# The output row in two 224-column halves on two column groups, and the last output weights in another order

## The chip, the cores and the metric

The kernel runs on one core of one Trainium2 chip. The metric is the device time of one execution in microseconds (us). Runs were made in sets of rounds: in each set the kernel before was run too, and a kernel is compared with the runs of the kernel before in its own set, because the kernel before itself has medians from 1284.22 to 1284.88 us in different sets. A ratio is the mean time of one kernel's runs over that of the other's of the same rounds, so it is not quite the ratio of the medians quoted beside it.

## The reference, cut to what matters

One token attends to a long cache, and a gated feed-forward branch is mixed in.

```python
# x: 1x448; k_cache, v_cache: 8 kv heads x 65536 x 256, bf16; wq: 448x4096; wo: 4096x448
q = (x @ wq) as 16 heads of 256           # 2 q heads share one kv head
p = softmax(q k^T / 16);  o = p v
a = o.reshape(4096) @ wo                  # 1x448
h = relu(x @ W_gate) * (x @ W_up)         # 1x1792
b = h @ W_down                            # 1x448
out = g * a + (1 - g) * b,  g = sigmoid(sum(x * gate_w))
```

The two caches are 2 x 268 MB, read once. Everything else is small.

## The kernel before: the parts that matter

K and V come in tiles of 8 MB (128 partitions x 64 KB) into a ring of three buffers. The order of the transfers on the one DMA queue is fixed by a list. The first K tile goes to buffer 0, the feed-forward weights to buffer 2, the second K tile to buffer 1. The third K tile needs buffer 2, so it can be issued only after the feed-forward products have been computed.

```python
order = [("wq", 0, 8.7), ("k", 0, TILE), ("gu", 0, 7.7), ("wd", 0, 3.8)]
for n in range(1, NT):
    order.append(("k", n, TILE))
    ...
slot, held, freed = {}, {2: ["gu", "dn"]}, {}      # buffer 2 is free after products gu and dn
...
PIECES = [(0, 64), (64, 96), (96, 112), (112, 120), (120, 128)]   # the last V tile in five pieces
for i, (lo, hi) in enumerate(PIECES):
    order.append(("vp", i, TILE * (hi - lo) / U))
WO = [(JL, 2 * NW), (2 * NW, J - 4), (J - 4, J - 2), (J - 2, J - 1), (J - 1, J)]
for i in range(1, 5):
    order.append(("wo", i, 0.55 * (WO[i][1] - WO[i][0])))
```

The w_down product (called dn) is 14 matmuls of one row by 448 columns. It opens the sum for the output row. The wo product closes it: per q head two matmuls, one in row 0 and one in row 32 of the same PSUM bank, except for the last head, where both go to row 0. ScalarE copies row 32 out early, and VectorE adds the two.

```python
def f_dn(e):
    for ft in range(FT):
        ins = e.matmul(A_ps[0:1, 0:D], hT[:, ft:ft + 1], wd_sb[:, ft, :], start=(ft == 0), ...)
...
r_ = 32 if s == 1 and j < J - 1 else 0
ins = e.matmul(A_ps[r_:r_ + 1, 0:D], attnT[:, c:c + 1], wo_sb[:, j, s, :], ..., tile_position=(0, r_))
...
f0 = op("ac", ..., lambda e: e.copy(a_sb, A_ps[32:33, 0:D]), ...)
f1 = op("dv", T_END, lambda e: e.tensor_tensor(fin_o, A_ps[0:1, 0:D], a_sb, ALU.add), [fin, f0])
```

The first three heads (JL = 3) use another layout of the attention output (attnL) and of the weights, which are loaded by eight transfers to 4 partitions each:

```python
for f in range(2):
    for i_ in range(4):
        dma(... wl_sb[32 * f + i_:32 * f + i_ + 13:4, :, :], wlv[f, i_] ...)
```

Of the kernel before, what the change touches and what calls it, by code (L numbers as in the profile page):

```python
# [7 lines left out]
F32 = mybir.dt.float32  # L8
# [4 lines left out]
ALU = AluOpType  # L13
# [11 lines left out]
class _Plan:  # L25
# [8 lines left out]
    def op(self, eng, key, fn, deps=()):  # L34
        o = _Op(eng, key, fn, deps)
        self.ops.append(o)
        return o

    def dma(self, eng, key, sem, fn, deps=()):
        if sem not in self.dsem:  # L40
            self.dsem[sem] = self.es.enter_context(self.nc.semaphore("d_" + sem))
        o = _Op(eng, key, fn, deps, dma=sem)
        self.ops.append(o)
        return o
# [46 lines left out]
def bass_gated_mix__gqa_block_cached__glu_gated_reglu__decode_kernel(  # L91
# [13 lines left out]
    H = A_k_cache.shape[1]  # L105
    S = A_k_cache.shape[2]
    DH = A_k_cache.shape[3]
    D = A_x.shape[2]
    F = B_W_gate.shape[1]
    NQ = A_wq.shape[1]  # L110
    J = 2 * H
# [11 lines left out]
    JL = 3  # L123
# [4 lines left out]
    with es:  # L128
# [5 lines left out]
        ptp = [sb("ptp%d" % i, [128, 1024], BF) for i in range(2)]  # L134
# [18 lines left out]
        attnT = sb("attnT", [128, H * 4], BF)  # L153
        attnL = sb("attnL", [128, 32], BF)
        hT = sb("hT", [128, FT], BF)
# [7 lines left out]
        fin_o = P_sb[0:1, 0:D]  # L163
        gw_row = ptp[1][0:1, 0:D]
        xeo = ptp[1][0:1, 448:704]
        qrep = ptp[1][:, 704:960]
        a_sb = ptp[H % 2][0:1, 0:2 * D].bitcast(F32)
        gtmp = ptp[0][0:1, 0:2 * D].bitcast(F32)

        wq3 = ring[2][:, 0:R3 * NQ]  # L170
# [6 lines left out]
        wd_sb = ring[2][:, 0:FT * D].rearrange("p (ft d) -> p ft d", ft=FT)  # L177
# [4 lines left out]
        A_ps = ps("A_ps", [128, 512], F32)  # L182
# [12 lines left out]
        op, dma = pl.op, pl.dma  # L195
# [9 lines left out]
        order = [("wq", 0, 8.7), ("k", 0, TILE), ("gu", 0, 7.7), ("wd", 0, 3.8)]  # L205
# [4 lines left out]
        NW = H - 3  # L210
# [2 lines left out]
        order.append(("wl", 0, 0.5))  # L213
        order.append(("wo", 0, 7.3))
        PIECES = [(0, 64), (64, 96), (96, 112), (112, 120), (120, 128)]
        for i, (lo, hi) in enumerate(PIECES):
            order.append(("vp", i, TILE * (hi - lo) / U))

        WO = [(JL, 2 * NW), (2 * NW, J - 4), (J - 4, J - 2), (J - 2, J - 1), (J - 1, J)]
        for i in range(1, 5):  # L220
            order.append(("wo", i, 0.55 * (WO[i][1] - WO[i][0])))
        t = 3.0
        tL, issue = {}, []
        for kind, i, d in order:
# [3 lines left out]
        T_END = t + 20.0  # L228
# [9 lines left out]
        wo_sb = ring[slot["wl", 0]][:, 0:J * 2 * D].rearrange("p (j s n) -> p j s n", j=J, s=2)  # L238
        wl_sb = ring[slot["wl", 0]][:, J * 2 * D:(J * 2 + JL * 8) * D].rearrange("p (j m) -> p j m", j=JL)
# [104 lines left out]
        def f_qk(n, b, sl):  # L344
# [12 lines left out]
                return ins  # L357
            return f

        l_, qk, smax, aexp, pv, last = {}, {}, {}, {}, {}, {}  # L360
        pending = []

# [61 lines left out]
        for kind, i, t in issue:  # L424
# [34 lines left out]
            elif kind == "wd":  # L459
                a3 = dma("sp", t, "wd", lambda e: e.dma_start(wd_sb, B_W_down.rearrange("(p ft) d -> p ft d", ft=FT)), [l_["q"]])  # L460

                def f_dn(e):
                    for ft in range(FT):
                        ins = e.matmul(A_ps[0:1, 0:D], hT[:, ft:ft + 1], wd_sb[:, ft, :], start=(ft == 0), stop=False,
                                       skip_group_check=True)
                    return ins
                l_["dn"] = op("pe", max(tg + 12.2, tL["wd", 0]), f_dn, [l_["hT"], a3])
            elif kind == "k":
# [14 lines left out]
                if t_ == NTH - 1:  # L483
# [12 lines left out]
                    ev = []  # L496
# [61 lines left out]
                        l_["wl"] = dma("sp", t + 0.01 * (4 * f + i_), "wl", lambda e, f=f, i_=i_: e.dma_start(  # L558
                            wl_sb[32 * f + i_:32 * f + i_ + 13:4, :, :], wlv[f, i_]), free(("wl", 0)))


        LAST = last["tn", H - 1]
        def f_wl(e):
            for j in range(JL):
                for s in range(8):
                    c = j // 2 * 16 + s * 2 + j % 2
                    ins = e.matmul(A_ps[0:1, 0:D], attnL[0:48, c:c + 1], wl_sb[0:48, j, s * D:(s + 1) * D],
                                   start=False, stop=False, skip_group_check=True, tile_position=(0, 0))
            return ins
        op("pe", max(tL["wo", 0], last["tn", NW - 1] + 0.5), f_wl,  # L570
           [l_["wl"], l_["dn"]] + [last["norml", h] for h in range((JL + 1) // 2)])
        for i, (lo, hi) in enumerate(WO):
            for h in range(lo // 2, (hi + 1) // 2):
                key = max(tL["wo", i], last["tn", h] + 0.5) + 0.01 * h
                if i in (1, 2):
                    key = LAST - (0.7, 0.2)[i - 1]
                elif i > 2:
                    key = LAST + 2 + 0.1 * i

                def f_wo(e, h=h, lo=max(lo, 2 * h), hi=min(hi, 2 * h + 2)):  # L580
                    for j in range(lo, hi):
                        for s in range(2):
                            c = h * 4 + s * 2 + j - 2 * h
                            r_ = 32 if s == 1 and j < J - 1 else 0
                            ins = e.matmul(A_ps[r_:r_ + 1, 0:D], attnT[:, c:c + 1], wo_sb[:, j, s, :],
                                           start=(s == 1 and j == JL), stop=(j == J - 1 or (j == J - 2 and s == 1)),
                                           skip_group_check=True, tile_position=(0, r_))
                    return ins
                fin = op("pe", key, f_wo, [l_["wo", i], last["norm", h], l_["dn"]])
                if i == 3:  # L590
                    f0 = op("ac", key + 0.01, lambda e: e.copy(a_sb, A_ps[32:33, 0:D]), [fin, last["ev", H - 2][1]])
        f1 = op("dv", T_END, lambda e: e.tensor_tensor(fin_o, A_ps[0:1, 0:D], a_sb, ALU.add), [fin, f0])
        f2 = dma("sp", T_END + 1, "out", lambda e: e.dma_start(out[0, :, :], fin_o), [f1])

        pl.serialize(touch_m)
        progs = pl.finish()
# [53 lines left out]
```

## Time and profile before

| what | value |
|---|---|
| median of 3 runs | 1284.27 us (1284.11 to 1284.40) |
| bytes read | 549 MB, mean 429 GB/s |
| busiest compute engine | VectorE, 49% |
| third K tile issued | 61.30 us |
| first piece of the last V tile: wait ends | 1266.19 us |
| output DMA issued | 1281.01 us |

From the page of the kernel before: the span from the first to the last instruction, engine busy time, then the row of the 40 slices for the DMA engines (9 is 90% or more) and the line of the main DMA queue.

```profile
span 1282.5 us, 10004 instructions
...
PE 431.5 (34%) x4636; PEld 163.4 (13%) x4636; DVE 634.4 (49%) x426; ACT 61.8 (5%) x116; POOL 4.1 (0%) x21
...
DMA  9999999999999999999999999999999999999998
...
q1 hardware_dynamic: 12674, 549.03, 99.3%
```

The reader sees a kernel bound by its transfers. No compute engine is near full. The Trainium skill (Perfetto Trace Analysis, "What 'DMA-bound' means") lists "Specific DMA engines" as the first thing that such a kernel can be bound on. This case agrees: the trace keeps 16 completion times for the last wo transfer, and they reach from 1271.27 to 1279.38. The mean over all 16 hides it.

Now the tail, from the timeline of the kernel before. Columns: start, duration, engine, line, operation, output<-inputs, shapes, count, and in brackets the idle time before it and what ended it.

```profile
1266.19 3.58 PE L376 MATMUL O<-ring,ptp 128*4 128x512 bf16 x32 [3.41 <-DMA ring<-in_A_v_cache_dram]
...
1274.81 0.60 PE L376 MATMUL O<-ring,ptp 128*4 128x512 bf16 x4 [0.21 <-DMA ring<-in_A_v_cache_dram]
1276.07 0.60 PE L376 MATMUL O<-ring,ptp 128*4 128x512 bf16 x4 [0.66 <-DMA ring<-in_A_v_cache_dram]
1276.72 0.69 DVE L387 CAST o_sb<-O 128x512 bf16<-128x512 f32 x1 [56.13 <-PE O L376]
...
1277.17 0.91 PE L585 MATMUL A_ps<-ring,attnT 128*1 128x448 bf16 x4 [0.50 <-DMA ring<-in_A_wo_dram]
...
1278.01 0.27 PE L392 MATMUL M_ps<-emat,o_sb 128*128 128x2 bf16 x4
...
1278.30 2.03 PE L585 MATMUL A_ps<-ring,attnT 128*1 128x448 bf16 x8
1278.31 0.16 DVE L396 TENSOR_TENSOR attnT<-M_ps,hs 128x4 bf16<-128x4 f32 x1 [0.90 <-PE M_ps L392]
...
1279.42 0.09 PEld L585 LDWEIGHTS A_ps<-ring,attnT 128*1 128x1 bf16 x2 [0.48 <-DMA ring<-in_A_wo_dram]
1279.62 0.52 ACT L591 COPY ptp<-A_ps 1x448 f32<-1x448 f32 x1 [59.15 <-PE A_ps L585]
1280.36 0.61 DVE L592 TENSOR_TENSOR P_sb<-A_ps,ptp 1x448 bf16<-1x448 f32 x1 [1.89 <-PE A_ps L585]
1281.01 0.28 SPq L593 DMA_DIRECT2D out_dram<-P_sb  x1
```

The last V piece is waited for until 1276.07. The normalised output of the last kv head (attnT) is ready at 1278.47. But the last wo head lands only at 1279.42, and after it come 1.59 us: matmuls, add, issue. So the last wo transfer ends the kernel.

And the start, from the timeline around 60 us (the SPq row is the issue of the third and fourth K tile):

```profile
58.46 2.81 PE L464 MATMUL A_ps<-ring,hT 128*1 128x448 bf16 x14
61.30 0.80 SPq L472 DMA_DIRECT2D ring<-in_A_k_cache_dram  x2
```

The issue follows the w_down product at once.

The table of stretches at the end of the kernel before (columns: stretch, its length, busy time and count of each engine, granted clock, DMA share, GB/s):

```profile
1277.00:1278.00 1.00, 0.83 (x4) 0.09 (x4) 0.41 (x1) 0.00 (x0) 0.00 (x0) 0.50 0.27 104
1278.00:1279.00 1.00, 0.98 (x11) 0.35 (x10) 0.16 (x1) 0.00 (x0) 0.00 (x0) 0.50 0.08 29
```

A share of 0.08 of 16 engines is one or two engines. Seven packets are in flight at 1277.0, three at 1278.0 and none at 1279.0, so a few stragglers set the last landing.

### The profile page before, as it was taken

To read this page: it belongs to the slowest core of one execution; us is meant where nothing else is said; L and a number is where in the kernel's file an instruction comes from. 1 tells how busy PE (TensorE), PEld (TensorE's weight loads), DVE (VectorE), ACT (ScalarE), POOL (GpSimd) and SP (SyncE) were. 2 spreads that over 40 slices of the span, in tenths; PEclk is the share of its full clock that TensorE was granted. 3 is DMA by queue.
4 is the path that set the end of the run, shared out by engine and by line. 5 is a ranking of instruction groups with operands and counts; after the bars stand their busy time and mean duration, and the time that the engine had idled before them with its cause. 6 is when DMAs were issued, how large, how long until landed. Compare 5 with 4: busy or idle time off the path is not lost.

```text
span 1282.5 us, 10004 instructions
## 1 busy us (share of the span) xinstructions
PE 431.5 (34%) x4636; PEld 163.4 (13%) x4636; DVE 634.4 (49%) x426; ACT 61.8 (5%) x116; POOL 4.1 (0%) x21
## 2 busy tenths in 40 slices
PE   3633332334123431225331243321433324233236
PEld 2401110111001110001110111100111101011011
DVE  2597633465534655434555444555435555335600
ACT  0001000000000000000000000000000000000000
POOL 1000000000000000000000000000000000000000
PEclk9656666656566665666655666656666655666576
DMA  9999999999999999999999999999999999999998
GB/s 398 424 426 436 440 427 432 443 427 426 438 440 430 428 430 437 434 434 424 436 438 432 427 438 436 426 429 444 430 426 434 438 431 430 440 428 432 436 413 328
DMA packets 12719, 549.67 MB, mean 429 GB/s; under 512 B 1315, under 2 KB 3238, under 8 KB 3718
## 3 DMA queue, kind: packets, MB, share of 16 engines
q1 hardware_dynamic: 12674, 549.03, 99.3%
q8 instruction: 36, 0.59, 0.2%
q14 instruction: 5, 0.04, 0.0%
q10 hardware_dynamic: 4, 0.00, 0.0%
HBM read 549.03 MB, written 0.00 MB: 428 GB/s over the span
## 4 chain that ended last, share of the span: by engine, by line
DVE 34%; DMA 32%; another core or an unknown queue 16%; PE 15%; SPq 1%; ACT 1%; issue 1%
DVE ring L342 30%; DMA ring<-in_A_k_cache_dram 27%; PE ST L354 6%; PE O L376 6%; DMA ring<-in_B_W_up_dram 3%; DMA ring<-in_A_wo_dram 2%; DVE P_sb L500 1%; SPq L541 1%; DVE nmb L478 1%; PE PT L505 1%; PE M_ps L448 1%; PE M_ps L451 0%; ACT ptp L514 0%; DVE o_sb L387 0%
## 5 line engine op out<-in xcount | busy, mean ns | idle before, releaser
L342 DVE STREAM_TRANSPOSE ring<-ring 128x2048 uint32<-128x2048 uint32 x256 | 565.4, 2274 | 411.5 <-DMA ring<-in_A_k_cache_dram 411.5
L354 PE MATMUL ST<-ring,xm 128*16 128x512 bf16 x2048 | 224.2, 612 | 753.0 <-DVE ring L342 753.0
L354 PEld LDWEIGHTS ST<-ring,xm 128*16 128x16 bf16 x2048 | 61.5, 120 | 902.4 <-DVE ring L342 793.4
L376 PE MATMUL O<-ring,ptp 128*4 128x512 bf16 x2048 | 147.7, 450 | 30.8 <-DMA ring<-in_A_v_cache_dram 26.8
L480 ACT ACTIVATE P_sb<-ST,nmb 128x512 bf16<-128x512 f32 x32 | 45.4, 1417 | 1114.0 <-DVE nmb L478 1114.0
L478 DVE TENSOR_REDUCE nmb<-ST 128x1 f32<-128x512 f32 x32 | 22.1, 689 | 110.0 <-PE ST L354 110.0
L376 PEld LDWEIGHTS O<-ring,ptp 128*4 128x4 bf16 x2048 | 54.8, 98 | 123.2 <-issue 55.0
L387 DVE CAST o_sb<-O 128x512 bf16<-128x512 f32 x8 | 5.5, 692 | 77.9 <-PE O L376 77.9
L500 DVE TENSOR_TENSOR P_sb<-P_sb,hs 128x1024 bf16<-128x1024 bf16 x16 | 18.9, 1221 | 8.7 <-ACT hs L494 8.7
L505 PE MATMUL PT<-identb,P_sb 128*128 128x128 bf16 x128 | 16.6, 311 | 15.5 <-DVE P_sb L500 14.7
L448 PE MATMUL M_ps<-xT,ring 128*128 128x1 bf16 x84 | 9.5, 205 | 17.8 <-DMA ring<-in_B_W_up_dram 17.8
L505 PEld LDWEIGHTS PT<-identb,P_sb 128*128 128x128 bf16 x128 | 12.3, 141 | 18.3 <-DVE P_sb L500 18.3
L514 ACT COPY ptp<-PT 128x256 bf16<-128x256 bf16 x32 | 10.4, 375 | 23.0 <-PE PT L505 23.0
L314 PE MATMUL M_ps<-ring,P_sb 128*128 128x256 bf16 x64 | 8.8, 309 | 3.1 <-DMA ring<-in_A_wq_dram 3.1
L448 PEld LDWEIGHTS M_ps<-xT,ring 128*128 128x128 bf16 x84 | 7.2, 151 | 18.4 <-issue 18.0
L480 ACT ACTIVATION_READ_ACCUMULATOR P_sb<-ST,nmb 128x1 f32 x32 | 8.5, 266 | 0.0
L451 PE MATMUL M_ps<-xT,ring 128*64 128x1 bf16 x56 | 7.8, 276 | 0.0
L314 PEld LDWEIGHTS M_ps<-ring,P_sb 128*128 128x128 bf16 x64 | 7.0, 111 | 4.6 <-issue 3.1
L431 DVE STREAM_TRANSPOSE ptp<-P_sb 128x128 uint32<-128x128 uint32 x1 | 0.3, 311 | 12.1 <-ACT P_sb L430 12.1
L490 PE MATMUL M_ps<-identf,hs 128*2 128x128 f32 x8 | 2.6, 322 | 10.0 <-DVE hs L488 10.0
L451 PEld LDWEIGHTS M_ps<-xT,ring 128*64 128x64 bf16 x56 | 5.4, 191 | 0.4
L526 DVE RECIPROCAL hs<-M_ps 128x2 f32<-128x2 f32 x8 | 1.4, 170 | 7.4 <-PE M_ps L525 7.4
(78 smaller groups left out, 72.9 us busy)
## 6 DMA issues: line engine op xcount, KB each, us to landing
ring<-in_A_v_cache_dram SPq DMA_DIRECT2D x1, 4096.0 KB, 29.6
ring<-in_A_wq_dram SPq DMA_DIRECT2D x1, 3072.0 KB, 10.3
ring<-in_A_v_cache_dram SPq DMA_DIRECT2D x1, 2048.0 KB, 25.0
ring<-in_B_W_down_dram SPq DMA_DIRECT2D x1, 1568.0 KB, 22.1
ring<-in_A_wo_dram SPq DMA_DIRECT2D x1, 1568.0 KB, 24.5
ring<-in_B_W_gate_dram SPq DMA_DIRECT2D x1, 1344.0 KB, 33.0
ring<-in_B_W_up_dram SPq DMA_DIRECT2D x1, 1344.0 KB, 35.6
ring<-in_A_v_cache_dram SPq DMA_DIRECT2D x1, 1024.0 KB, 26.9
```

What stands on the lines that cost most here:

```text
L314: ins = e.matmul(QN_ps, xw3[:, k_, 31 - j:159 - j], rhs, start=(j == 0 and kt == 0), stop=(j == J - 1 and kt == R3))
L342: return lambda e: e.transpose(v, v)
L354: ins = e.matmul(bank[32 * w:32 * w + 16, :], xm[:, x0:x0 + 16], ktv[sl][:, u0:u0 + 16, c, :, r_], start=(b == 0 and c == 0 and r_ == 0), ...
L376: ins = e.matmul(OP[h % 2][32 * g:32 * g + 4, :], ptp[h % 2][:, col:col + 13:4], ring[sl][:, k * 512:(k + 1) * 512], start=(a == 0 and k < ...
L448: e.matmul(GU_ps[:, c:c + 1], wf3[which][:, kt * F + ft:(kt + 1) * F:FT], xT[:, kt:kt + 1], start=(kt == 0), stop=False, skip_group_check= ...
L451: ins = e.matmul(GU_ps[64 * half:64 * half + 64, c:c + 1], wfh[which][:, ft:F // 2:FT], xT[:, R3 + half:R3 + half + 1], start=False, stop= ...
L478: smax[n] = op("dv", tk + 22, lambda e, n=n, NM=NM, t_=t_: e.tensor_reduce(NM[:, t_:t_ + 1], ST[n % 2][:], AX.X, ALU.max, negate=True), [q ...
L480: aexp[n] = op("ac", tk + 23, lambda e, n=n, t_=t_, NM=NM, RS=RS: e.activation(P_sb[:, t_:2048:4], ST[n % 2][:], ACTF.Exp, bias=NM[:, t_:t ...
L500: rsc = op("dv", tt, lambda e, X=X, pb=pb: e.tensor_tensor(pb, pb, X[:, 12:16].unsqueeze(1).to_broadcast([128, 256, 4]), ALU.mult), [h7, a ...
L505: ins = e.transpose(PT[rd][:, s * 128:(s + 1) * 128], P_sb[:, (rd * 8 + s) * 128:(rd * 8 + s + 1) * 128], identb[:, :])
L514: ins = e.copy(dst, src)
L541: dep = dma("sp", t, "vp%d" % i, lambda e, sl=sl, n=n, lo=lo, hi=hi: e.dma_start(ring[sl][:, lo * 256:hi * 256], v_src(n)[:, lo * 256:hi * ...
```

## The change

The intent: shorten what follows the last bytes. Every product into the output row is cut into two halves of 224 columns, which go to two column groups of TensorE and overlap. The two halves are copied out by VectorE and ScalarE side by side, instead of one add after the other. Two wo heads are loaded ahead of the last V piece, and the last four heads come one per transfer.

```diff
-        WO = [(JL, 2 * NW), (2 * NW, J - 4), (J - 4, J - 2), (J - 2, J - 1), (J - 1, J)]
-        for i in range(1, 5):
-            order.append(("wo", i, 0.55 * (WO[i][1] - WO[i][0])))
+        WO = [(JL, 2 * NW), (J - 6, J - 4)] + [(j, j + 1) for j in range(J - 4, J)]
         for i, (lo, hi) in enumerate(PIECES):
+            if i == len(PIECES) - 1:
+                order.append(("wo", 1, 1.1))
             order.append(("vp", i, TILE * (hi - lo) / U))
+        for i in range(2, 6):
+            order.append(("wo", i, 0.55))
...
+        D2 = D // 2
+        def proj(e, lhsT, rhs, start, stop):
+            for g in range(2):
+                ins = e.matmul(A_ps[32 * g:32 * g + 1, 0:D2], lhsT, rhs[:, g * D2:(g + 1) * D2], start=start, stop=stop,
+                               skip_group_check=True, tile_position=(0, 32 * g))
+            return ins
...        # w_down, attnL and wo products: each old matmul becomes one proj(...)
-        f1 = op("dv", T_END, lambda e: e.tensor_tensor(fin_o, A_ps[0:1, 0:D], a_sb, ALU.add), [fin, f0])
+        f0 = op("dv", T_END, lambda e: e.tensor_copy(fin_o[:, 0:D2], A_ps[0:1, 0:D2]), [fin])
+        f1 = op("ac", T_END, lambda e: e.copy(fin_o[:, D2:D], A_ps[32:33, 0:D2]), [fin])
```

More of the change, by code (lines that the diff above doesn't have):

```diff
@@ L166, in bass_gated_mix__gqa_block_cached__glu_gated_reglu__decode_kernel @@
         qrep = ptp[1][:, 704:960]
-        a_sb = ptp[H % 2][0:1, 0:2 * D].bitcast(F32)
         gtmp = ptp[0][0:1, 0:2 * D].bitcast(F32)
@@ L463, in f_dn @@
                     for ft in range(FT):
-                        ins = e.matmul(A_ps[0:1, 0:D], hT[:, ft:ft + 1], wd_sb[:, ft, :], start=(ft == 0), stop=False,
-                                       skip_group_check=True)
+                        ins = proj(e, hT[:, ft:ft + 1], wd_sb[:, ft, :], ft == 0, False)
                     return ins
@@ L566, in f_wl @@
                     c = j // 2 * 16 + s * 2 + j % 2
-                    ins = e.matmul(A_ps[0:1, 0:D], attnL[0:48, c:c + 1], wl_sb[0:48, j, s * D:(s + 1) * D],
-                                   start=False, stop=False, skip_group_check=True, tile_position=(0, 0))
+                    ins = proj(e, attnL[0:48, c:c + 1], wl_sb[0:48, j, s * D:(s + 1) * D], False, False)
             return ins
@@ L574, in bass_gated_mix__gqa_block_cached__glu_gated_reglu__decode_kernel @@
                 key = max(tL["wo", i], last["tn", h] + 0.5) + 0.01 * h
-                if i in (1, 2):
-                    key = LAST - (0.7, 0.2)[i - 1]
-                elif i > 2:
+                if i in (2, 3):
+                    key = LAST - (0.7, 0.2)[i - 2]
+                elif i > 3:
                     key = LAST + 2 + 0.1 * i
@@ L583, in f_wo @@
                             c = h * 4 + s * 2 + j - 2 * h
-                            r_ = 32 if s == 1 and j < J - 1 else 0
-                            ins = e.matmul(A_ps[r_:r_ + 1, 0:D], attnT[:, c:c + 1], wo_sb[:, j, s, :],
-                                           start=(s == 1 and j == JL), stop=(j == J - 1 or (j == J - 2 and s == 1)),
-                                           skip_group_check=True, tile_position=(0, r_))
+                            ins = proj(e, attnT[:, c:c + 1], wo_sb[:, j, s, :], False, j == J - 1 and s == 1)
                     return ins
                 fin = op("pe", key, f_wo, [l_["wo", i], last["norm", h], l_["dn"]])
-                if i == 3:
-                    f0 = op("ac", key + 0.01, lambda e: e.copy(a_sb, A_ps[32:33, 0:D]), [fin, last["ev", H - 2][1]])
-        f1 = op("dv", T_END, lambda e: e.tensor_tensor(fin_o, A_ps[0:1, 0:D], a_sb, ALU.add), [fin, f0])
-        f2 = dma("sp", T_END + 1, "out", lambda e: e.dma_start(out[0, :, :], fin_o), [f1])
+        f0 = op("dv", T_END, lambda e: e.tensor_copy(fin_o[:, 0:D2], A_ps[0:1, 0:D2]), [fin])
+        f1 = op("ac", T_END, lambda e: e.copy(fin_o[:, D2:D], A_ps[32:33, 0:D2]), [fin])
+        f2 = dma("sp", T_END + 1, "out", lambda e: e.dma_start(out[0, :, :], fin_o), [f0, f1])
         pl.serialize(touch_m)
```

## The prediction

> **What bounds the kernel.** It streams 549 MB at a mean of 429 GB/s; the page's slice table shows DMA at 9 tenths or more in all slices but the last (8). No other engine is over 49% busy. So only what follows the last bytes, or a DMA gap, can move the time.
>
> **The tail now (timeline).** The last V piece is waited for until 1276.07; its PV matmuls take 0.60, the cast 0.69 (from 1276.72). The first late wo transfer lands at 1277.12, and its four 448-column matmuls (0.91) hold the transposing matmuls back until 1278.01. attnT is ready at 1278.47. PE then waits for wo until 1278.85 and 1279.42. After that last landing come the last head's two 448-column matmuls on one column group, one after the other (to 1280.33 = 0.91), VectorE's 448-wide add (1280.36, 0.61) and the output DMA at 1281.01.
>
> The stretch table shows the DMA share falling to 0.27 at 1277, 0.08 at 1278, 0 at 1279: one or two of the 16 engines finish about 2 us late and gate each landing. The Trainium skill (DMA: Bandwidth & Descriptors, "Why a DMA increments its semaphore by 16 and not by 1") says only the full count of 16 means that all data landed; the trace agrees: landings continue while the share is near 0.1.
>
> **What the change does.**
> 1. Transfers: same bytes, one transfer more. 448 KB goes ahead of the last V piece, which lands about 1.1 us later: about 1277.15. Single heads land at about 1277.7, 1278.3, 1278.85, 1279.42 (0.57 apart, as before). The last landing does not move.
> 2. V chain from 1277.15: PV 0.60, cast 0.69, transposing matmuls 0.3, attnT 0.16: ready about 1279.0, still ahead of the last landing. Head 12 runs during the cast, 13 and 14 between 1278.8 and 1279.6.
> 3. Last head: four 224-column matmuls in two pairs. A 448-column one takes 0.35 at clock 0.5; pairs on two column groups overlap (14 in 1.49 us, 0.106 each, against 24 on one group in 4.70, 0.196 each, both at clock 1.0). Estimate 2x0.18+0.2 = 0.55 instead of 0.91; queued behind 13 and 14, PE ends near 1280.0 instead of 1280.33.
> 4. Final copy: 224 columns on VectorE and ScalarE in parallel. Estimates: VectorE 0.38 (from the 512-column cast's 0.69), ScalarE 0.36 (from the 448-column copy's 0.52), instead of 0.61: 0.2 less. The early 448-wide ScalarE copy (0.52) was beside the path; removing it is worth nothing.
> Sum: 0.3+0.2 = about 0.5 us.
>
> Off the path: the attnL product (4.70, now perhaps 2.5 to 4) hides behind V pieces. The w_down product (2.6 at 58.66) precedes the issue of two K tiles at 61.30 and gets up to 1 us shorter; most DMA engines start new packets only after 62.0, but the slowest still works on the old tile until about 64 (first transpose 64.2), and it sets the end. I count nothing for this.
>
> **Prediction:** 1283.7 us, 8 in 10 between 1283.0 and 1284.3. Faster by over 2%: 0.005; within 2%: 0.99; slower: 0.005.
>
> **What would show it.** Last wo wait ending at the same time within 0.5 us, last V piece about 1 us later; PE's last four matmuls about 0.55; final copies under 0.42 each, starting together; output DMA issued near 1280.5.
>
> **What would make it wrong.** The V chain ends last instead of wo (up to +0.5); the extra transfer or its blocked issue (issues were held up to 10.6 us) delays the last landing; the two copies of one PSUM bank slow each other; or the earlier K issue moves the slowest DMA engine too (0.5 to 1 us gained).

## The result

The changed kernel took 1285.38 us in the median (1283.94 to 1285.84, 4 runs), the kernel before 1284.34 (1284.11 to 1284.97) in the same rounds; ratio 1.0005, 95% interval 0.9988 to 1.0023. Within 2%, as forecast, but 1.7 us above the predicted 1283.7 and outside the range of 1283.0 to 1284.3. Its single runs also scatter over 1.9 us, against 0.9 for the kernel before.

The same lines of the page, for the changed kernel:

```profile
span 1283.1 us, 10133 instructions
...
PE 427.8 (33%) x4700; PEld 164.4 (13%) x4700; DVE 634.3 (49%) x426; ACT 61.5 (5%) x116; POOL 4.1 (0%) x21
...
DMA  9999999999999999999999999999999999999997
...
q1 hardware_dynamic: 12690, 549.03, 99.3%
```

The same bytes and the same share of the DMA queue. The span is 0.5 us longer (1283.06 against 1282.53 in the traces), but the device times of these two profiled runs, 1285.20 and 1284.32, are 0.88 apart; I come back to the rest below. The timeline of its tail shows more:

```profile
1267.17 3.58 PE L386 MATMUL O<-ring,ptp 128*4 128x512 bf16 x32 [6.92 <-DMA ring<-in_A_v_cache_dram]
...
1275.76 0.60 PE L386 MATMUL O<-ring,ptp 128*4 128x512 bf16 x4 [0.54 <-DMA ring<-in_A_v_cache_dram]
...
1278.15 0.60 PE L386 MATMUL O<-ring,ptp 128*4 128x512 bf16 x4 [0.35 <-DMA ring<-in_A_v_cache_dram]
...
1278.80 0.69 DVE L397 CAST o_sb<-O 128x512 bf16<-128x512 f32 x1 [57.69 <-PE O L386]
...
1279.55 0.27 PE L402 MATMUL M_ps<-emat,o_sb 128*128 128x2 bf16 x4 [0.31 <-DVE o_sb L397]
...
1279.75 1.32 PE L366 MATMUL A_ps<-ring,attnT 128*1 128x224 bf16 x12
1279.85 0.16 DVE L406 TENSOR_TENSOR attnT<-M_ps,hs 128x4 bf16<-128x4 f32 x1 [0.36 <-PE M_ps L402]
1280.13 0.49 PEld L366 LDWEIGHTS A_ps<-ring,attnT 128*1 128x1 bf16 x8 [0.30 <-DMA ring<-in_A_wo_dram]
...
1280.40 0.22 PEld L366 LDWEIGHTS A_ps<-ring,attnT 128*1 128x1 bf16 x4
...
1281.11 0.34 ACT L595 CAST P_sb<-A_ps 1x224 bf16<-1x224 f32 x1 [60.12 <-PE A_ps L366]
1281.11 0.38 DVE L594 CAST P_sb<-A_ps 1x224 bf16<-1x224 f32 x1 [1.09 <-PE A_ps L366]
1281.54 0.28 SPq L596 DMA_DIRECT2D out_dram<-P_sb  x1
```

(The row at 1280.40 is from the same timeline, asked from 1280.35 on. It is the second half of the row at 1280.13, which merges two heads: the first four weight loads waited for attnT, the last four for the last wo head, which landed at 1280.36.)

Take the first row and the last of the two tails. From the first piece of the last V tile to the issue of the output DMA: 1281.01 - 1266.19 = 14.82 us before, 1281.54 - 1267.17 = 14.37 us after. I call this difference the tail. The tail became 0.45 us shorter. But the tail began 0.98 us later. So the tail did what it was meant to do, and in these two profiles 0.98 us were lost in the stream, before any instruction that the change meant to speed up.

A second loss lies outside the span. Device time less span is 2.10 to 2.31 us in every run of the changed kernel, and 1.75 to 1.86 in every run of the kernel before whose span is on record. That is about 0.36 us more, in every run, and it takes back most of the 0.45 gained in the tail. The column "outside" of the table below shows it.

And the start of the changed kernel, beside the rows shown of before:

```profile
58.28 1.52 PE L366 MATMUL A_ps<-ring,hT 128*1 128x224 bf16 x28
59.84 0.80 SPq L481 DMA_DIRECT2D ring<-in_A_k_cache_dram  x2
```

The w_down product takes 1.52 us instead of 2.81, and the third K tile is issued 1.46 us earlier. Nevertheless that tile landed later. The next rows are VectorE's first transposes of the third K tile; first the kernel before:

```profile
83.56 4.50 DVE L342 STREAM_TRANSPOSE ring<-ring 128x2048 uint32<-128x2048 uint32 x2 [1.69 <-DMA ring<-in_A_k_cache_dram]
```

then the changed kernel:

```profile
84.64 4.50 DVE L343 STREAM_TRANSPOSE ring<-ring 128x2048 uint32<-128x2048 uint32 x2 [2.85 <-DMA ring<-in_A_k_cache_dram]
```

A transfer issued 1.46 us earlier landed 1.08 us later. The trace also records every DMA packet with its start and duration, though not its engine. A 64 KB packet of a K or V tile normally takes 2.42 us. Counting the packets in flight at a moment gives the number of engines at work (a 17 is an overlap of a few nanoseconds). "Idle" is the engine time without a packet between 58 and 66 us, summed over 16 engines; "slow" is the time above 2.42 us of the 64 KB packets that start between 60.8 and 68 us.

```
profiled run         issue  engines at work at 60.5 61 61.5 62 62.5 63 63.5 64 64.5 65   idle  slow  slowest packet
before               61.30                     16  16   6   3  12  15   16  16  16  16   14.6   8.7  3.28
after                59.84                     16  16  16  13  13  14   16  16  17  16    4.4  19.8  3.94
```

Before, most engines run dry by 61.5 and start again together near 62.3, while one late engine is still on the second tile. Their first packets take about 3 us. The late engine starts its first packet of the third tile at 63.69, when that burst is over, and that packet is not slow (none that starts after 63.1 takes over 2.5 us). After, the engines start at different times between 61.1 and 63.6, their packets take 2.8 to 3.94 us, and the slowest is one that starts as late as 63.43. This was my reading of one pair of traces. It gave the theory to be tested. Idle and slow together are 23.3 us before and 24.2 after, about 1.5 us for each engine in both, so what could differ is which engine is hit.

### The profile page after: what moved, and what is told of

It reads as the page before. It is cut to its first block, busy times and chain, and to the rows that moved or that the text cites. A ratio compares the mean times of both kernels' runs of the same rounds, so it can differ in the third digit from the quotient of the medians.

```text
span 1283.1 us, 10133 instructions
## 1 busy us (share of the span) xinstructions
PE 427.8 (33%) x4700; PEld 164.4 (13%) x4700; DVE 634.3 (49%) x426; ACT 61.5 (5%) x116; POOL 4.1 (0%) x21
## 4 chain that ended last, share of the span: by engine, by line
DVE 34%; DMA 32%; another core or an unknown queue 16%; PE 15%; SPq 1%; ACT 1%; issue 1%
DVE ring L343 30%; DMA ring<-in_A_k_cache_dram 27%; PE ST L355 7%; PE O L386 6%; DMA ring<-in_B_W_up_dram 3%; DMA ring<-in_A_v_cache_dram 2%; DVE P_sb L509 1%; SPq L550 1%; DVE nmb L487 1%; PE PT L514 1%; PE M_ps L458 1%; PE M_ps L461 0%; DVE o_sb L397 0%; ACT ptp L523 0%
```

## The experiments

Theory C: the shorter w_down product moves the issue of the third K tile into the moment when some DMA engines are dry and others are not; the late engines are then slowed, and the stream ends late and at a time that scatters. Rivals: the change slows the stream in another way, through its transfers (B2), its number of instructions (B1, D), or not at all, and the difference is chance (A, D).

All runs gave the correct result. In the table, "diff" is the difference of the mean of a kernel's runs and of the kernel before in the same set, "range" the spread of its single runs, "tail" as defined above, "issue", "idle" and "slow" as above (of the profiled run). "Outside" is device time less span, the mean over all runs of the kernel; for the kernel before it is 1.80 or 1.81 in every set. The range of the kernel before was 0.59, 0.85, 1.09, 2.04 and 0.88 us in the five sets; the 2.04 comes from one run of 1286.34.

| run | median | diff | range | tail | issue | idle | slow | outside |
|---|---|---|---|---|---|---|---|---|
| after_again | 1284.58 | +0.44 | 2.26 | 14.40 | 60.71 | 10.6 | 9.1 | 2.20 |
| halves_only | 1284.02 | -0.05 | 0.97 | 14.23 | 60.64 | 9.7 | 10.6 | 2.20 |
| transfers_only | 1284.99 | +0.55 | 1.61 | 14.96 | 62.12 | 28.2 | 9.0 | 1.82 |
| after_wl8 | 1293.42 | +9.00 | 2.79 | 14.34 | 59.60 | 4.8 | 19.5 | 2.19 |
| after_dnserial | 1284.55 | -0.53 | 1.09 | 14.37 | 60.30 | 5.5 | 13.5 | 2.16 |
| after_dnearly | 1283.48 | -1.48 | 0.50 | 14.28 | 59.14 | 6.3 | 7.1 | 2.17 |
| before_dnearly | 1285.36 | +0.34 | 2.73 | 14.82 | 59.60 | 4.3 | 15.1 | 1.80 |
| after_jl4 | 1285.87 | +1.30 | 2.50 | 14.34 | 59.28 | 4.7 | 11.3 | 2.17 |
| after_same_chip | 1285.18 | +0.25 | 2.77 | 14.23 | 60.16 | 7.0 | 18.2 | 2.18 |
| dnserial_same_chip | 1284.63 | +0.24 | 2.72 | 14.28 | 60.47 | 9.1 | 9.1 | 2.16 |
| dnearly_same_chip | 1283.64 | -1.09 | 0.21 | 14.38 | 58.36 | 0 | 1.0 | 2.17 |
| halves_dnearly | 1283.56 | -1.25 | 0.40 | 14.22 | 58.24 | 0 | 0.7 | 2.20 |
| before_dnpair | 1285.68 | +0.72 | 2.49 | 14.80 | 60.24 | 8.1 | 21.0 | 1.81 |
| before_pad64 | 1285.21 | -0.04 | 1.00 | 14.81 | 61.15 | 11.4 | 11.7 | 1.84 |
| after_dnlong | 1285.47 | +0.62 | 0.78 | 14.38 | 62.91 | 38.4 | 8.1 | 2.19 |
| before_dnpair_early | 1283.81 | -1.08 | 0.55 | 14.82 | 58.66 | 0 | 1.0 | 1.82 |
| halves_dnearly_2 | 1283.52 | -1.19 | 0.26 | 14.23 | 57.51 | 0 | 0 | 2.18 |
| halves_dnearly_jl2 | 1282.99 | -1.59 | 1.33 | 14.12 | 58.56 | 0 | 2.5 | 2.01 |

The column "outside" separates the kernels cleanly. All kernels with the halves and the shared copy have 2.0 to 2.2 us, all others 1.8. The transfers (transfers_only, 1.82), the overlapping w_down product (before_dnpair, 1.81) and the number of instructions (before_pad64, 1.84, with 10132 instructions like halves_only) are not the cause. Why the halves cost this time, no run shows.

### First set: which part of the change costs

**after_again** is the changed kernel, no edit.

> The changed kernel once more, unaltered. Theory A (the end is set by the slowest of 16 DMA engines, whose lag depends on which engines the instruction fetches and the attnL-weight load fall on; the change itself only shortens the tail): in the profile, the time from the first wait of the last V tile's first piece to the issue of the output DMA is again 14.4 +-0.2 us (14.82 in the kernel before, 14.38 in the first profile of the changed one), while that first piece's landing lies anywhere between 1265.5 and 1267.5. Times between 1283.5 and 1286. Rival B (the change slows the stream by about 1 us every time): the landing is again at 1267.2 +-0.3 and the median 1285.4 +-0.3.

Median 1284.58 (1283.61 to 1285.87), before 1284.22 (1283.99 to 1284.58); ratio 1.0003. The tail was 14.40, and the first piece was waited for until 1266.50. So the tail is steady, and the stream's end is not: rival B's fixed 1267.2 falls, as theory A said. In this set, as in the others, the changed kernel against the kernel before is not clear of noise.

**halves_only** keeps the halves and the shared copy and takes back the transfers:

```diff
-        WO = [(JL, 2 * NW), (J - 6, J - 4)] + [(j, j + 1) for j in range(J - 4, J)]
+        WO = [(JL, 2 * NW), (2 * NW, J - 4), (J - 4, J - 2), (J - 2, J - 1), (J - 1, J)]
```

> Two halves on two column groups and the shared copy, with the transfers of the kernel before. Theory A: last head about 0.55 us instead of 0.91 and copies 0.38 instead of 0.61, so from the landing of the last wo head to the output DMA's issue about 1.0 us instead of 1.59; from the first piece of the last V tile to that issue about 14.2 us. Rival B1 (more PE instructions, 129 in all, or the earlier release of ring 2 slow the stream): first piece lands about 1 us later than 1266.2 and the median is about 1284.8 to 1285.4.

The end of its timeline:

```profile
1279.24 0.09 PEld L364 LDWEIGHTS A_ps<-ring,attnT 128*1 128x1 bf16 x4 [0.28 <-DMA ring<-in_A_wo_dram]
1279.83 0.34 ACT L593 CAST P_sb<-A_ps 1x224 bf16<-1x224 f32 x1 [57.55 <-PE A_ps L364]
1279.83 0.38 DVE L592 CAST P_sb<-A_ps 1x224 bf16<-1x224 f32 x1 [1.52 <-PE A_ps L364]
1280.26 0.28 SPq L594 DMA_DIRECT2D out_dram<-P_sb  x1
```

From the last landing to the issue 1280.26 - 1279.24 = 1.02 us, against 1.59 before: as expected. The tail is 14.23, also as expected. Yet its mean is only 0.05 us below that of the kernel before, and its runs scatter over 0.97 us against 0.59. Of the gain of 0.59 in the tail, 0.39 are lost outside the span. The 0.15 us that are still missing are no more than noise, so this run alone shows no loss in the stream.

**transfers_only** is the kernel before with the new order and sizes of the transfers, and the old matmuls and add.

> The order and sizes of the last transfers of the changed kernel, with the old matmuls and the old add. Theory A: the last V piece is waited for 2.3 us after the one before it, as in the changed kernel (1.26 in the kernel before), attnT gets ready last, PE then needs three heads with the last one serial (about 1.3 to 1.6 us) and the add 0.61, so from the first piece of the last V tile to the output DMA's issue 14.9 to 15.2 us, and the median 0 to 0.5 us above the kernel before. Rival B2 (the reordered, smaller transfers slow the stream): first piece and last landing both about 1 us later, median 1285.5 or more.

The end of its timeline:

```profile
1277.98 0.59 PE L378 MATMUL O<-ring,ptp 128*4 128x512 bf16 x4 [0.35 <-DMA ring<-in_A_v_cache_dram]
...
1281.30 0.61 DVE L594 TENSOR_TENSOR P_sb<-A_ps,ptp 1x448 bf16<-1x448 f32 x1 [1.46 <-PE A_ps L587]
1281.94 0.28 SPq L595 DMA_DIRECT2D out_dram<-P_sb  x1
```

The tail is 14.96, 0.14 longer than before and in the expected range. So the new order by itself loses a little: the last V piece lands 1.1 us later, and its chain, not the last wo head, then ends last. The mean, 0.55 above before, is more than the tail explains. Its profiled run happened to issue the third K tile at 62.12 (the first product after the first K tile took 6.46 us), and its engines were idle for 28 us in sum. The mean of the 16 completions of the third K tile is 83.55, 0.75 us later than in the kernel before (82.80), and that of the last wo head is still 0.76 us later (1277.01 against 1276.25). So in this profile the dry spell accounts for the 0.8 us by which the stream ended late; the mean of the five runs is not clear of noise.

**after_wl8** loads the attnL weights to 8 neighbouring partitions per transfer:

```diff
-                            wl_sb[32 * f + i_:32 * f + i_ + 13:4, :, :], wlv[f, i_]), free(("wl", 0)))
+                            wl_sb[32 * f + 8 * i_:32 * f + 8 * i_ + 8, :, :], wlv[f, i_]), free(("wl", 0)))
```

(with `wlv` rearranged to match, and two transfers per f instead of four)

> The changed kernel with the attnL weights loaded by 4 transfers of 8 partitions instead of 8 of 4. Theory A: these 8x84 KB go to 4 DMA engines only (24 packets of 0.27 us = 6.5 us on each), and the slowest of the four ends last; over 8 engines it is 3.3 us each, the gate passes to the engines with instruction fetches, and the end comes 0.5 to 1.3 us earlier: median 1284.0 to 1284.8, landing of the first piece of the last V tile near 1266. Rival B: no change against the changed kernel (1285.4), as the same bytes are loaded.

A miss: 9 us slower. The 7 KB packets of these transfers took 0.49 us in the median, up to 0.88, against 0.27 in the changed kernel, and large packets of other transfers were slowed meanwhile (up to 5.5 us). The Trainium skill (DMA: Bandwidth & Descriptors, "The descriptor swizzle") gives the SBUF port by groups of four neighbouring partitions, so four engines would write one port at once here, and each its own port with the old stride of 4. The durations fit that, but no run separates it, so it is argued, not shown. The run changed two things at once and does not answer its question.

### Second and third set: moving the issue

**after_dnserial** orders the 28 half matmuls of the w_down product by column group, so that they don't overlap:

```diff
-                    for ft in range(FT):
-                        ins = proj(e, hT[:, ft:ft + 1], wd_sb[:, ft, :], ft == 0, False)
+                    for g in range(2):
+                        for ft in range(FT):
+                            ins = e.matmul(A_ps[32 * g:32 * g + 1, 0:D2], ...)
```

> The changed kernel, with the w_down product's 28 half matmuls ordered by column group (14 on one, then 14 on the other), so that they don't overlap and take about 2.6 us again instead of 1.52; nothing else differs. Theory C (the shorter w_down product issues the third and fourth K tile 1.1 us earlier, 59.8 to 60.7 instead of 61.3, while one DMA engine still has its last packet of the second tile before it; the restart then slows that engine's packets and it stays about 1 us late to the end): issue at 61.2 to 62.2, no slow packet on the late engine, first piece of the last V tile lands at 1266.2 +-0.4, median 1283.7 to 1284.2. Rival D (the lag comes only from where instruction fetches fall, one fetch more among them): median stays at 1284.6 to 1285.2.

The product took 2.47 us, but the issue came at 60.30, not at 61.2 or later: the product ahead of it happened to take 5.15 us (granted clock 0.73), where it took 5.49 in the kernel before (0.67). So the run did not make the condition that it was meant to. The mean was 0.53 below before here and 0.24 above in the repetition (dnserial_same_chip), whose runs scatter over 2.72 us. Inconclusive: as a test of theory C this is a miss.

**after_dnearly** puts the w_down product between the two halves of the first K tile's scores, which frees buffer 2 earlier. Only the sort keys of three operations change:

```diff
-                l_["relu"] = mop("dv", tg + 12, ...
-                l_["hT"] = mop("dv", tg + 12.1, ...
-                l_["dn"] = op("pe", max(tg + 12.2, tL["wd", 0]), ...
+                l_["relu"] = mop("dv", tg + 9.3, ...
+                l_["hT"] = mop("dv", tg + 9.4, ...
+                l_["dn"] = op("pe", max(tg + 9.5, tL["wd", 0]), ...
```

> The changed kernel with the w_down product placed between the two halves of the first K tile's scores instead of after both. Theory C: the third K tile is issued near 57.5, before any DMA engine runs dry at about 61, so there is no restart with 3 us packets at 61 to 64, and the stream ends 0.5 to 1.7 us earlier than in the kernel before: first piece of the last V tile at 1264.5 to 1265.7, median 1282.3 to 1283.4. Rival D: nothing changes against the changed kernel, median 1284.6 to 1285.2. Rival E (any earlier issue only hurts): median above 1285.

1283.48 (1283.32 to 1283.82), all five runs below all nine of the kernel before (1284.62 to 1285.47). The first piece was waited for until 1265.77. The rival theories D and E fall. Theory C's own numbers (median at most 1283.4, first piece at most 1265.7) were missed by less than 0.1 us. In the profiled run the issue was at 59.14, later than hoped, and some engines were still dry for a moment (6.3 us in sum).

**before_dnearly** is the same edit on the kernel before.

> The kernel before with the same move of the w_down product alone. Theory C: issue near 58.6, still before the engines run dry at 61; first piece of the last V tile 0.5 to 1.7 us earlier than 1266.2, median 1282.7 to 1283.8. Rival D: median stays at 1284.2.

A miss: 1285.36, with a range of 2.73 us. Its w_down product still takes 2.8 us and more (the first 12 of its 14 matmuls take 2.84), so the issue came at 59.60, and the trace shows the worst of both: not all engines kept busy (idle 4.3) and slow packets (15.1 us in sum, up to 4.09). An issue that is earlier but not early enough did not help here; with this scatter, that it hurts is not shown.

**after_jl4** has four heads instead of three in the attnL layout (`JL = 4`).

> The changed kernel with four heads instead of three in the attnL layout, whose weights go to 4 of the 16 DMA engines. If those four engines end last (theory A), they get 8 packets of 0.27 us more and all engines 0.57 us less: the end comes 1.0 to 1.6 us later, median 1285.9 to 1286.6, first piece of the last V tile near 1268.3. If the engines that take instruction fetches end last, the end comes 0.5 us earlier: median 1284.4 or less.

1285.87, with a mean 1.30 above before; the three sets of the changed kernel are 0.69, 0.44 and 0.25 above. So about 0.8 us later than the changed kernel, a little under the 1.0 to 1.6 expected if the four engines with these weights end last. In its trace the last of them ends these packets at 1253.71, and the other engines end the tile before at 1249.99 or earlier. The Trainium skill (DMA: Bandwidth & Descriptors, "Why a DMA increments its semaphore by 16 and not by 1") says that a transfer is split over the largest number of engines, up to 16, that divides its slowest dimension on both sides. The trace agrees for 4 partitions: in the kernel before, the 96 packets of these weights form four back-to-back chains of 24.

**after_same_chip**, **dnserial_same_chip**, **dnearly_same_chip** and **halves_dnearly** were run together. The first three repeat kernels from above; the last is halves_only with the edit of after_dnearly.

> The changed kernel unaltered, on one chip with the next three. Theory C (the shorter w_down product moves the issue of the third K tile and makes the stream end about 1 us later): 0.3 to 1.0 us above the kernel before, and 0.7 to 1.5 above the next kernel. Theory D (the stream's end is a lottery of DMA engine lags, no part of the change moves it): equal to the next kernel within 0.4 us.

> The changed kernel with the w_down product's halves ordered by column group, on the same chip. Theory C: median 0.3 to 0.7 us below the kernel before. Theory D: as the changed kernel, within 0.4 us.

> The changed kernel with the w_down product between the halves of the first K tile's scores, on the same chip. As found on the other chip: 1.0 to 1.6 us below the kernel before, and spread under 0.7 us. If that was chance of that chip: within 0.4 us of the changed kernel.

> A candidate that takes the halves and the shared copy, the transfers of the kernel before, and the early w_down product. The tail from the first piece of the last V tile to the output DMA's issue should be 14.2 us (as with the halves alone) against 14.3 to 14.4 with the changed transfers, so 0.1 to 0.2 us below the kernel above: 1.1 to 1.8 us below the kernel before.

Changed kernel: 1285.18 (1283.72 to 1286.49). With the early w_down product: 1283.64 (1283.55 to 1283.76), and with the old transfers besides 1283.56 (1283.26 to 1283.66). Before: 1284.82 (1284.05 to 1285.14). So the gain is not of one set, and the scatter falls from 2.77 us to 0.21. The repetition of dnserial went against theory C, which had expected it 0.7 to 1.5 us below the changed kernel: the two means differ by 0.02 us, as D said. Its issue was at 60.47, not later than 61, so again the condition was not made.

The start of halves_dnearly, from its timeline (the SPq row covers the issue of both tiles; the first is at its start):

```profile
56.41 1.61 PE L364 MATMUL A_ps<-ring,hT 128*1 128x224 bf16 x24
...
58.24 2.16 SPq L479 DMA_DIRECT2D ring<-in_A_k_cache_dram  x2
```

and the arrival of its third K tile:

```profile
82.95 4.51 DVE L341 STREAM_TRANSPOSE ring<-ring 128x2048 uint32<-128x2048 uint32 x2 [1.70 <-DMA ring<-in_A_k_cache_dram]
```

The issue is 3 us earlier than before, the landing 0.6 us earlier (1.7 against the changed kernel). No engine runs dry.

### Fourth set: the w_down product alone

The prediction had failed in the stream; was it the w_down product or the number of instruction fetches?

**before_dnpair** is the kernel before with one thing changed: the 14 w_down matmuls alternate between two column groups and overlap.

```diff
-                        ins = e.matmul(A_ps[0:1, 0:D], hT[:, ft:ft + 1], wd_sb[:, ft, :], start=(ft == 0), ...)
+                        r_ = 32 * (ft % 2)
+                        ins = e.matmul(A_ps[r_:r_ + 1, 0:D], hT[:, ft:ft + 1], wd_sb[:, ft, :], start=(ft < 2), ...,
+                                       tile_position=(0, r_))
```

(and the wo product no longer opens row 32 itself)

> The kernel before with one thing changed: the 14 matmuls of the w_down product alternate between two column groups, so they overlap and take about 1.5 us instead of 2.8; same instructions, same transfers, same tail. Theory C (the earlier issue of the third K tile is what costs the changed kernel): issue near 60.0 to 60.7 instead of 61.3; times scatter over more than 1.2 us, median 0.3 to 1.0 us above the kernel before; tail from the last V tile's first piece to the output DMA's issue 14.8 as before. Rival D: equal to the kernel before within 0.3 us and as narrow.

1285.68 (1284.23 to 1286.72), a mean 0.72 above before. In its timeline:

```profile
58.67 1.53 PE L465 MATMUL A_ps<-ring,hT 128*1 128x448 bf16 x14
60.24 0.80 SPq L473 DMA_DIRECT2D ring<-in_A_k_cache_dram  x2
```

The tail is 14.80, as before. The numbers are those that theory C expected and not those of rival D. But the loss is not clear of noise by itself: the interval of the ratio is 0.9992 to 1.0018, and the kernel before scattered over 2.04 us in this set, by one run. The sure result comes from the comparison with before_dnpair_early below: the same matmuls, placed earlier, take 1.79 us less, and every run of one kernel is below every run of the other.

**before_pad64** adds 64 one-column matmuls to the kernel before, into an unused row, in V tiles 4 to 11:

```diff
+                for _ in range(8 if n in range(4, 12) else 0):
+                    e.matmul(A_ps[64:65, 0:1], ptp[h % 2][:, a:a + 1], ptp[h % 2][:, a:a + 1], start=True, stop=True, ...)
```

> The kernel before with 64 one-column matmuls into an unused row of the output bank, 8 in each of 8 V tiles, so that it has the changed kernel's number of instructions (about 10130) and its 37 instruction fetches. Theory C: equal to the kernel before within 0.3 us. Rival D (the fetches make the difference): 0.5 to 1.0 us above, scattered like the changed kernel.

The page counts 37 instruction packets, as in the changed kernel, against 36. The mean is 0.04 below before (the median 0.41 above), the range 1.00 us. So no loss from one instruction fetch more is seen. Its profile is a warning, though: with the issue at 61.15, as in the kernel before, a late engine took 3.62 us for a packet that started at 64.9, and the third K tile was waited for until 85.77, later than in any profile of the changed kernel. So a late engine can be slowed without the earlier issue too.

**after_dnlong** makes the w_down product serial and adds 10 wide matmuls to an unused row behind it, so that the issue comes later than before:

```diff
+                    for _ in range(10):
+                        ins = e.matmul(A_ps[64:65, 0:D], hT[:, 0:1], wd_sb[:, 0, :], start=True, stop=True, ...)
```

> The changed kernel with the w_down product serial and followed by 10 wide matmuls into an unused row, so that the third K tile is issued near 62.3, when nearly all DMA engines have run dry. Theory C: the engines restart together, so the times scatter less (range under 0.8 us) than the changed kernel's 1.9 to 2.8, but all engines lose about 1 us: median 0.0 to 0.6 us above the kernel before. Rival D: as the changed kernel, range over 1.5 us.

1285.47 (1285.12 to 1285.90). With all engines dry (idle 38.4 us in sum) and a common restart, the runs scatter over 0.78 us instead of 2 to 3, but all are late: the median is 0.67 above before, where theory C had at most 0.6. Of the mean of 0.62 above, 0.39 lie outside the span, and the tail is 0.44 shorter than before (14.38 against 14.82), so the stream ended about 0.7 us later.

**before_dnpair_early** joins before_dnpair and before_dnearly.

> The kernel before with the paired w_down product, placed between the two halves of the first K tile's scores; tail and transfers as before. Theory C: the third K tile is issued at 58.5 or earlier, no DMA engine runs dry, no slow packets at 61 to 66; median 0.7 to 1.2 us below the kernel before, range under 0.6 us. Rival D: equal to the kernel before within 0.3 us.

1283.81 (1283.49 to 1284.04), every run below every run of the kernel before (1284.30 to 1286.34). The same pair of column groups that stood 0.72 us above before on its own gains 1.08 us where it lets the issue come in time. The tail of this kernel is the old one, so the gain owes nothing to the halves of the output row. The engines at work, counted as above, for the runs that span the range:

```
profiled run         issue  engines at work at 60.5 61 61.5 62 62.5 63 63.5 64 64.5 65   idle  slow  slowest packet
before_dnpair_early  58.66                     16  16  17  16  16  16   16  16  16  16    0     1.0  2.98
halves_dnearly       58.24                     16  16  16  16  16  16   16  17  16  16    0     0.7  2.78
before_dnpair        60.24                     16  15  15  12  12  14   14  15  16  16    8.1  21.0  3.71
transfers_only       62.12                     16  13   6   3   2   0   13  15  16  16   28.2   9.0  3.25
after_dnlong         62.91                     16  16  11   3   2   1    0   5  14  16   38.4   8.1  3.36
```

### Fifth set: the better version

**halves_dnearly_2** repeats halves_dnearly, and **halves_dnearly_jl2** is the same with `JL = 2`.

> The best version so far once more, on the chip of the next run: 1.0 to 1.4 us below the kernel before, range under 0.6 us.

> The same with two heads instead of three in the attnL layout, whose weights go to 4 of the 16 DMA engines. In the trace of the version above one of these four ends last (1251.3 us against 1249.7 for the others, before the last V tile). 8 packets of 0.27 us less on the four and 0.57 us more on all should end the stream 0.5 to 1.0 us earlier if instruction fetches late in the run don't make another engine the last: 0.3 to 1.0 us below the version above. If another engine is last: 0 to 0.5 us above it.

1283.52 (1283.31 to 1283.57) and 1282.99 (1282.54 to 1283.87), against 1284.82 (1284.15 to 1285.03) before. Each run of both is below each run of the kernel before. The second, with ratio 0.9988 (interval 0.9975 to 1.0000), is the best version found; against the first its median gains 0.53 us, in the expected range, though one of its runs is above them all. About 0.17 us of this lie outside the span (2.01 against 2.18), which was not expected. In its trace the last engine ends the attnL weights at 1248.85, and not at 1251.19 as in halves_dnearly_2.

## Why the prediction was wrong

1. **What bounds the kernel**: right within the span, where all of the loss and gain is in the DMA stream or after it. The 0.36 us outside the span were not foreseen.
2. **Step 1, the transfers**: the last V piece was to land 1.1 us later relative to the stream. It did: from the first piece of the last V tile to the last piece 9.88 us before (1276.07 - 1266.19) and 10.98 after. "The last landing does not move" was also right relative to the stream: PE's last wait for wo ends 13.23 us after the first piece of the last V tile in both (1279.42 - 1266.19 and 1280.40 - 1267.17). In absolute time it is 0.98 us later, because the end of the stream was late.
3. **Step 2, the V chain**: attnT was to be ready "about 1279.0, still ahead of the last landing". Right, again relative to the stream: 1280.01, still 0.35 us ahead of the last landing (1280.36). But the matmuls of the last two heads then queue on TensorE, and the profile's chain of waits runs back through the last V piece. So the new order gained nothing: halves alone have a tail of 14.23, halves and transfers 14.23 to 14.40.
4. **Step 3, the last head**: right in kind. From the end of the last wait to the start of the final copy it is 0.71 us (1281.11 - 1280.40) instead of 0.94 (1280.36 - 1279.42), 0.23 less where 0.3 was counted. Pairs of halves overlap: 28 of 224 columns took 1.52 us, where 14 of 448 took 2.81. The Trainium skill (TensorEngine Tiling (Array Packing), "Key Properties") says that tiles can run weight loads and matmuls in parallel; the trace agrees with these numbers.
5. **Step 4, the copies**: right. 0.38 and 0.34 us, started together, where 0.38 and 0.36 had been estimated. The two reads of one PSUM bank did not slow each other.
6. **The sum of 0.5 us**: right for the tail: 0.45 in the first pair of profiles, 0.42 to 0.59 in the later profiles of the changed kernel. But the sum stopped at the issue of the output DMA. That is the first step that failed: the time outside the span was taken as unchanged, and it grew by 0.36 us in every run. What the halves gain in device time is therefore only about 0.1 to 0.2 us.
7. **The second step that failed**, and the larger one in the set of the result, is the sentence on the w_down product: it "gets up to 1 us shorter; most DMA engines start new packets only after 62.0, but the slowest still works on the old tile until about 64 (first transpose 64.2), and it sets the end. I count nothing for this." The first half is measured (1.3 us shorter, issue at 59.84 to 60.71 instead of 61.30). The conclusion was wrong. I saw the dry spell and took it for harmless, and in the list of risks I gave an earlier issue only a gain. What the issue at about 60 costs in the stream is the "diff" plus the gain in the tail, less the 0.36 outside the span where the kernel has the halves: 0.8, 0.5 and 0.5 us for the three sets of the changed kernel, 0.2 for halves_only, and 0.7 for before_dnpair. The mean is 0.5 with a standard error of about 0.2 (my estimate from the scatter of the runs), so that it costs anything is likely, not certain. Counted the same way, the five kernels with the overlapping product placed early (JL = 3, issue at 59.14 or earlier) gain 1.0 to 1.3 us, with ranges of 0.2 to 0.6 us, and this is clear of noise.

   The 16 completion times of a transfer, taken here as one for each engine, show how both fit together. Their mean, for the third K tile and then for the last wo head, is 82.80 and 1276.25 in the kernel before, 82.87 and 1276.41 in the changed kernel, and 81.4 to 81.6 and 1275.0 to 1275.2 in four kernels that never ran dry (dnearly_same_chip, halves_dnearly, halves_dnearly_2, before_dnpair_early). What the dry spell costs the engines in the mean is thus still there 1200 us later, and the changed kernel lost almost nothing in the mean. It lost at one engine: the latest completion moved from 1279.38 to 1280.36, 2.06 us behind the second latest (0.76 before). In both profiles it comes 27.1 us after the last completion of the attnL weights, which only four engines carry (1252.26 before, 1253.26 after). The same distance, within 0.1 us, is found in 15 of the 17 profiles with these weights (JL = 3, without after_wl8). So as a rule the latest of these four ends the stream. That this one was made late by the restart at 61 to 64 is argued: the trace does not name the engines.

In the set of the result, the mean was 0.69 us above before, where 0.64 below was predicted: 0.8 us were lost in the stream and 0.36 outside the span, and the tail gave 0.45.

With the w_down product early, the same tail change gave 1283.48 and 1283.64 in two sets, within the predicted range. That is luck and no proof of the prediction: before_dnpair_early, with the old tail, is in the range too (1283.81). The arithmetic of the tail itself was sound up to the output DMA's issue.

What stays open: the changed kernel's mean was 0.69, 0.44 and 0.25 above before in three sets. Even taken together they are not clearly slower than the kernel before (0.46 with a standard error of about 0.26, my estimate); only that the predicted gain of 0.6 us is missing is sure. Theory C fits the sign and the scatter of the loss in the stream, but the profile of one run does not predict its end: after_again landed its third K tile at 85.27, later than the first profile's 84.64, and still ended earlier. The lags of the 16 engines change again later, with instruction fetches among other things. The origin of the 0.36 us outside the span is open.

## What to carry to other kernels

In a kernel that streams at the limit of its DMA engines, look first at every place where a transfer waits for compute, and ask whether the queue still holds work for all engines at that moment. Here a faster product helped surely only where the issue then came before most engines ran dry; halfway there it gained nothing and probably cost something. Judge a change of half a microsecond at the tail by a difference within one profile (here, from one landing to the last issue), and the whole time by several sets of runs. Then compare span and device time: here most of what the span gained in the tail was lost outside it.

## What the Trainium skill lacked or had wrong

- **DMA: Bandwidth & Descriptors** does not say what a restart costs. After a dry spell most of the first 64 KB packets took 2.8 to 3.3 us each instead of 2.42, and single ones up to 3.9 to 4.1 us where the engines started one after the other. Without the dry spell they took 2.42 to 3.13, most of them 2.42.
- **DMA: Bandwidth & Descriptors**, "Where 436 GB/s comes from", says that for HBM to SBUF the HBM side, at about 358 GB/s per core, binds. Here one core read 549 MB from HBM at a mean of 429 GB/s, and a 64 KB packet took 2.42 us, which is 27.1 GB/s per engine and 433 GB/s on 16. Taken alone the sentence misleads for a core that streams alone; the page's own measured figures, given there for one core alone, reach about the same rate as this run.
- **Runtime: NRT & Kernel Launch**, "Instruction fetch mechanics", tells how instructions are fetched by DMA, but not what this costs a stream of data. In the kernel before, 36 packets of 16 KB came with about 10000 instructions. Each took about 1.07 us, where a data packet of that size takes 0.61 us. Late in the stream the engines were far apart: half of them completed one tile between 1108.13 and 1110.21, and the other half 4.6 to 6.7 us after the first. That the fetches did this is argued, as the trace does not name the engines.
- **DMA: Bandwidth & Descriptors**, "The descriptor swizzle", gives the ports but no cost of sharing one; **SBUF — State Buffer** has rates by the number of ports that one transfer reaches, but not what such a transfer does to the packets of others in flight. Here packets of 7 KB took 0.49 us in the median to 8 neighbouring partitions, against 0.27 us to 4 partitions at a stride of 4, and 64 KB packets of other transfers took up to 5.5 us meanwhile; that the port is the reason was not separated from the rest.
